# Splitting one float32 load of v in two, with its scalings, two w_out combinations and one turn put elsewhere in two queues

## The chip, the cores and the metric

One core of one Trainium2 chip runs the whole program. The metric is device time in microseconds (us), lower is better. The profile is of one execution of the same program, taken by the hardware profiler; its engines are PE (matmul), PEld (weight loads into PE), DVE (vector), ACT (activations), POOL (GpSimd) and SP (which computes nothing and issues DMAs).

## The reference

Retention over 4 sequences of 768 tokens with 8 heads of 64, then a feed-forward layer with a sine in it, over the 3072 tokens.

```python
gamma = 1.0 - 2.0 ** (-5.0 - np.arange(H))
for t in range(S):
    state = gamma * state + einsum('bhd,bhe->bhde', k[:, :, t], v[:, :, t])
    y[:, :, t] = scale * einsum('bhd,bhde->bhe', q[:, :, t], state)
x = y.transpose(0, 2, 1, 3).reshape(B * S, H * D)
h = x @ w_in                       # 512 -> 2048
s = np.sin(alpha * h)
out = (h + s * s / (alpha + 1e-09)) @ w_out
```

## The kernel before, in words

**Tiles and phases.** Each sequence is cut into 6 chunks of 128 tokens, 24 in all, and these are worked off in the order of the list `order` (L70 to L74), called `P` later. P[11], the twelfth tile, is chunk 3 of the second sequence (sequence 1 in the code); P[12] and P[13] are its chunks 4 and 5. P[14], P[15] and P[16] are chunks 1 to 3 of the third sequence (sequence 2), P[17] is chunk 1 of the fourth (sequence 3). The tiles form ten groups (4, then eight times 2, then 4). Phase g (`phase`, L908) runs, for the tiles of group g, the product with `w_in` (L617), the sine and the square on ACT (L620, L625) and the sum on DVE into `gT` (L632), while PE also runs the product with `w_out` of group g-1 (L641). A phase of two tiles has 8 slots, n = 0 to 7. A place such as (3, 5) is slot 5 of phase 3. Functions put on a place by `at` run in that slot in the order in which they were put there; those put there by `mixes` run behind it.

**The burst of a tile.** At fixed places PE interrupts the feed-forward work with a burst (`burst`, L465): the state's share of the old tile's output (L380), the scores of the new tile (L402, L406), the sum of k times v of the old tile into the state (L428), and the old tile's own share (L444). For a tile that is `wide` (L128: from chunk 3 of the second sequence on) L428 and L444 read `v_seq`, the scaled v; the scores read `qkT`, the turned q and k. Old and new tile of the bursts that matter here are P[10] and P[11] at (3, 1), P[11] and P[12] at (3, 5), P[12] and P[13] at (4, 1), P[13] and P[14] at (4, 5), P[14] and P[15] at (5, 1), P[15] with P[16] and P[17] at (5, 6). PE runs its instructions in the order written, so when one waits, all behind it wait.

**How q, k and v of a wide tile arrive.** `load_seq` (L131) loads one sequence, or a `part` of its wide tiles, with eight DMAs, one for each pair of a half and a head. q and k go through POOL's queue into `qk_seq` (as bfloat16), v goes through SP's queue into the float32 buffer `vf`. `scale_v` (L191) then multiplies v of one tile by its decays on POOL, `vf` to `v_seq` (L197). `turn` (L301) is a transposing DMA in SP's queue, `qk_seq` to `qkT` (L304). `mix_w` (L675) forms one piece of a sum or difference of two blocks of `w_out` on POOL (L686), needed from phase 7 on. SP also issues the stores of results, `out_dram<-o_sb` (L654).

**What sets the order.** Everything is written out by hand: the place table `where` and the calls of `at` decide at which point of the program an instruction is issued, and each engine runs its own in that order. A DMA waits, before it is issued, for the DMA that was issued eight before it on the same engine (eight semaphores go round on each of the two engines), and for the data that it reads. Nothing behind a waiting instruction on its engine goes ahead. The function `loads` (L1134), at (2, 2), is the part that the change takes apart.

Of the kernel before, what the change touches and what calls it, by code (L numbers as in the profile page):

```python
# [38 lines left out]
def kernel(  # L39
# [55 lines left out]
    def half(x):  # L95
        return slice(64 * x, 64 * x + 64)

    def head(b, m, e):
        return 4 * m + 2 * e + (e ^ b)
# [28 lines left out]
    def wide(j):  # L128
        return j >= NCH + 3 and j % NCH > 0

    def load_seq(bt, names="qkv", part=slice(None), between={}, some=slice(None)):  # L131

        cs = [c for c in range(NCH) if wide(bt * NCH + c)]
        nh = 2 * len(cs)
        if ("seq", bt) not in raw:
            raw["seq", bt] = (big.tile([128, nh, 2, NP, D], BF16, name=f"qk_seq{bt}", tag=f"qk_seq{bt}"),
                              big.tile([128, nh, NP, D], BF16, name=f"v_seq{bt}", tag=f"v_seq{bt}"))
        tqk, tv = raw["seq", bt]
        now = cs[part]
        fs = slice(2 * (now[0] - cs[0]), 2 * (now[-1] - cs[0]) + 2)  # L140
        if "v" in names and "vf" not in raw:
            raw["vf"] = work.tile([128, 16, NP, D], F32, name="vf", tag="gA", bufs=1)
        for name, src in (("q", q), ("k", k), ("v", v)):
            if name not in names:
                continue
            if name == "v":
                vf = raw["vf"][:, 6:16] if bt == 2 else raw["vf"][:, 0:nh]
                for i, c in enumerate(cs):
                    raw["vf", bt * NCH + c] = vf[:, 2 * i:2 * i + 2]
            for n, (b, m, e) in list(enumerate(heads))[some]:  # L150
                if n in between:
                    between[n]()
                r, at = half(b), 2 * m + e
                o = vf[r, fs, at, :] if name == "v" else tqk[r, fs, "qk".index(name), at, :]
                (nc.sync if name == "v" else nc.gpsimd).dma_start(out=o, in_=src[bt, head(b, m, e), now[0] * C:(now[-1] + 1) * C, :].rearrange("(f i) d -> i f d", i=64))  # L155
        for i, c in enumerate(cs):
            j, f = bt * NCH + c, slice(2 * i, 2 * i + 2)
            raw["qk", j], raw["k", j], raw["v", j] = tqk[:, f], tqk[:, f, 1], tv[:, f]
# [32 lines left out]
    def scale_v(j, eng):  # L191
        t, by = raw["v", j], kg
        o = t
        if wide(j):
            o, t = (x.rearrange("i f p d -> i (f p) d") for x in (t, raw["vf", j]))
            by = kgq
        eng.tensor_mul(o, t, by[:, j % NCH, :, None].to_broadcast([128, H, D]))  # L197
# [103 lines left out]
    def turn(j):  # L301

        st["qkT", j] = work.tile([128, 2 * NP, 128], BF16, name="qkT", tag="qkT", bufs=6)
        nc.sync.dma_start_transpose(out=st["qkT", j], in_=raw["qk", j].rearrange(  # L304
            "i a f p d -> i (a f p d)" if wide(j) else "i a h d -> i (a h d)"))
# [369 lines left out]
    def mix_w(eng, home):  # L675

        n, i, c = w_todo[home].pop(0)
        a, b, op = W_MIX[n]
        if home == "vr":
            to = big.tile([128, 2, NH], BF16, name="w_mix", tag="vr", bufs=11)  # L680
        else:
            if home not in w_home:
                w_home[home] = (consts if home == "dec" else big).tile(
                    [128, 2 if home == "dec" else 3, 4, NH], BF16, name="w_mix", tag="dec" if home == "dec" else "qk_seq1")
            to = w_home[home][:, (2 if home == "dec" else 3) - 1 - len(w_todo[home])]
        eng.tensor_tensor(to, w_block(*a, slice(i, i + c)), w_block(*b, slice(i, i + c)), op=op)  # L686
        for j in range(c):
            w_mix[n, i + j] = to[:, j]
# [262 lines left out]
    def X(j):  # L951
        return lambda: turn(j)
# [3 lines left out]
    P = order  # L956
# [122 lines left out]
    def pieces_w(n, home):  # L1079
        return lambda: [mix_w(nc.gpsimd, home) for _ in range(n)]  # L1080

    def scaled(*js):
        return lambda: [scale_v(j, nc.gpsimd) for j in js]
# [5 lines left out]
    where = {}  # L1089
# [8 lines left out]
    def at(place, fn):  # L1098
        atts[place[0]].setdefault(place[1], []).append(fn)

    def B(old, new, first, beside, second):

        return lambda: burst(old, new, first, beside=beside, second=second)

    for n in range(9, 17):
        new = P[n]
        first = new - 1 if new % NCH == 1 else None
        at(where[n], B(P[n - 1], new, first, P[17] if n == 16 else None, e3 if n == 15 else None))
        if n != 10:
            at({15: (4, 6), 16: (4, 5)}.get(n, where[n]), X(P[n + 2]))  # L1110
    for i, spot in ((16, (6, 4)), (18, (7, 4)), (20, (8, 1))):
        new = P[i + 2:i + 4] if i < 20 else P[22:23]
        at(spot, lambda i=i, new=new: pair(P[i:i + 2], new))
# [19 lines left out]

    def loads():  # L1134
        turn(P[12])
        load_seq(1, "v")
        pieces_w(2, "vr")()
        scale_v(P[10], nc.gpsimd)
        pieces_w(2, "vr")()
        load_seq(2, "q")  # L1140
        load_seq(2, "k", between={4: scaled(P[11]), 5: pieces_w(1, "vr"), 7: pieces_w(1, "vr")})
        scale_v(P[12], nc.gpsimd)
        scale_v(P[13], nc.gpsimd)
        load_seq(3, "qk", slice(0, 2))

    at((2, 2), loads)
    def mixes(place, fn):
        behind_slot.setdefault(place, []).append(fn)

# [2 lines left out]
    for spot in ((4, 0), (4, 2)):  # L1152
        mixes(spot, lambda: mix_w(nc.vector, "vr"))
    for spot, fn in (((3, 6), pieces_w(2, "dec")), ((3, 6), scaled(P[14], P[15], P[16])), ((4, 5), pieces_w(1, "vr")),
                     ((4, 5), pieces_w(3, "seq"))):
        mixes(spot, fn)
    for spot, m, only in (((6, 1), 0, "s"), ((6, 3), 2, "s"), ((6, 3), 0, "dx"), ((6, 3), 2, "d"), ((6, 5), 4, "s"), ((6, 5), 2, "x"),
                          ((6, 5), 4, "dx"), ((6, 7), 6, "s"), ((6, 7), 6, "dx")):
        mixes(spot, lambda m=m, only=only: mix_g(6, m, 2, nc.gpsimd, only))
# [38 lines left out]
```

## Time and profile before

| | us |
|---|---|
| median of the 3 runs shown | 210.84 |
| the 3 runs | 210.84, 205.76, 210.92 |
| the profiled execution | 206.72 |
| its span (first to last instruction) | 205.0 |
| PE busy in the span | 197.3 (96%) |
| POOL busy | 177.7 (87%) |
| DVE busy | 159.1 (78%) |
| ACT busy | 153.5 (75%) |

The profiled execution lies 0.96 above the lowest run and 4.12 below the median. All positions below are from the start of its span. A row of the timeline gives start, length, engine, line, operation, what is written from what, and how many instructions were merged; the brackets at its end give the engine's idle time before it and what ended that. "DMA to landing" is the time from the start of a DMA's issue to the moment its last byte is reported there.

### The profile page before, as it was taken

To read this page: it belongs to the slowest core of one execution; us is meant where nothing else is said; L and a number is where in the kernel's file an instruction comes from. 1 tells how busy PE (TensorE), PEld (TensorE's weight loads), DVE (VectorE), ACT (ScalarE), POOL (GpSimd) and SP (SyncE) were. 2 spreads that over 40 slices of the span, in tenths; PEclk is the share of its full clock that TensorE was granted. 3 is DMA by queue.
4 is the path that set the end of the run, shared out by engine and by line. 5 is a ranking of instruction groups with operands and counts; after the bars stand their busy time and mean duration, and the time that the engine had idled before them with its cause. 6 is when DMAs were issued, how large, how long until landed. Compare 5 with 4: busy or idle time off the path is not lost.

```text
span 205.0 us, 6219 instructions
## 1 busy us (share of the span) xinstructions
PE 197.3 (96%) x2503; PEld 136.3 (67%) x2503; DVE 159.1 (78%) x340; ACT 153.5 (75%) x316; POOL 177.7 (87%) x212
## 2 busy tenths in 40 slices
PE   7889999999999999699999999999999999999994
PEld 7545544467776666466766666768888885555983
DVE  5788499877999977578788787796799896577853
ACT  7779788557997787667876959788777979999120
POOL 8999986999999799899999999899997997997000
DMA  8999999999999989999999799995063111001123
GB/s 131 151 181 193 199 201 175 167 131 129 109 184 186 115 153 146 208 166 109 183 172 225 79 131 186 187 213 133 25 80 83 28 51 56 0 0 51 54 102 102
DMA packets 104348, 26.52 MB, mean 129 GB/s; under 512 B 93648, under 2 KB 102528, under 8 KB 104320
## 3 DMA queue, kind: packets, MB, share of 16 engines
q0 software_dynamic: 66384, 11.67, 76.3%
q1 hardware_dynamic: 37936, 14.47, 35.7%
q8 instruction: 19, 0.31, 0.7%
q14 instruction: 9, 0.07, 0.2%
HBM read 27.30 MB, written 6.29 MB: 164 GB/s over the span
## 4 chain that ended last, share of the span: by engine, by line
PE 71%; DVE 14%; DMA 5%; ACT 4%; POOL 3%; issue 2%; SPq 0%; POOLq 0%; DVEq 0%
PE ph L617 32%; PE po L641 20%; DVE gT L632 6%; PE a L765 6%; DMA out_dram<-o_sb 3%; PE b L765 3%; PE ab L765 3%; DMA qkr<-in_k_dram 2%; ACT s L620 2%; ACT s L625 1%; PE c L765 1%; POOL qkr L125 1%; DVE xT L502 1%; DVE aTw L414 1%; PE py L380 1%
## 5 line engine op out<-in xcount | busy, mean ns | idle before, releaser
L632 DVE SCALAR_TENSOR_TENSOR gT<-s,rec_alpha,ph 128x256 bf16<-128x256 f32 (+3 forms) x164 | 79.5, 522 | 25.8 <-ACT s L625 24.4
L617 PE MATMUL ph<-xT,w_in 128*128 128x256 bf16 (+3 forms) x656 | 98.3, 291 | 0.4 <-DVE o_sb L651 0.2
L620 ACT ACTIVATE s<-ph,alpha_sb 128x256 f32<-128x256 f32 (+3 forms) x164 | 75.8, 505 | 26.0 <-PE ph L617 25.4
L617 PEld LDWEIGHTS <-w_in 128*128 128x128 bf16 x656 | 63.0, 98 | 27.2 <-issue 1.2
L625 ACT ACTIVATE s<-s 128x512 f32<-128x512 f32 (+1 forms) x94 | 58.7, 626 | 2.8
L641 PE MATMUL po<-w_out,gT 128*128 128x512 bf16 x224 | 58.3, 380 | 0.0
L719 POOL TENSOR_TENSOR g_mix<-gT 128x512 bf16<-128x512 bf16 (+1 forms) x51 | 49.2, 997 | 4.2 <-DVE gT L632 2.9
L641 PEld LDWEIGHTS <-gT 128*128 128x128 bf16 x224 | 20.4, 98 | 16.5 <-DVE gT L632 0.5
L155 POOL DMA_DIRECT2D qk_seq<-in_k_dram x32 | 21.5, 742 | 2.6 <-DMA qk_seq<-in_q_dram 2.5
L765 PEld LDWEIGHTS <-g_mix 128*128 128x128 bf16 x208 | 19.5, 98 | 4.7
L155 POOL DMA_DIRECT2D qk_seq<-in_q_dram x32 | 21.5, 725 | 0.0
L686 POOL TENSOR_TENSOR w_mix<-w_out 128x512 bf16<-128x512 bf16 (+1 forms) x13 | 20.0, 1606 | 0.0
L197 POOL TENSOR_TENSOR v_seq<-vf,kgq 128x512 bf16<-128x512 f32 x13 | 13.8, 1093 | 0.0
L125 POOL DMA_DIRECT2D vr<-in_v_dram x11 | 10.3, 934 | 1.5 <-DMA w_in<-in_moe_w_in_dram 1.3
L414 DVE TENSOR_TENSOR aTw<-pa,maskq 128x768 bf16<-128x768 f32 x10 | 9.6, 955 | 1.9 <-PE pa L428 1.7
L899 PE MATMUL spare<-warm 128*128 128x112 bf16 (+1 forms) x54 | 8.2, 324 | 1.2 <-DVE warm L207 1.2
L502 DVE TENSOR_TENSOR xT<-py,qg 128x512 bf16<-128x512 f32 x13 | 8.9, 685 | 0.5 <-PE py L460 0.5
L765 PEld LDWEIGHTS <-gT 128*128 128x128 bf16 x88 | 7.9, 98 | 1.9
L651 DVE COPY o_sb<-po 128x512 f32<-128x512 f32 x11 | 7.6, 690 | 1.6 <-PE po L641 1.1
L765 PE MATMUL a<-w_mix,gT 128*128 128x256 bf16 (+1 forms) x72 | 8.7, 261 | 0.0
L398 DVE TENSOR_TENSOR aT<-pa,mask 128x1024 bf16<-128x1024 f32 x7 | 8.5, 1220 | 0.1
L765 PE MATMUL b<-w_out,g_mix 128*128 128x256 bf16 x64 | 8.5, 273 | 0.0
(135 smaller groups left out, 225.2 us busy)
## 6 DMA issues: line engine op xcount, KB each, us to landing
out_dram<-o_sb SPq DMA_DIRECT2D x21, 256.0 KB, 4.4
w_in<-in_moe_w_in_dram POOLq DMA_DIRECT2D x8, 256.0 KB, 7.8
w_out<-in_moe_w_out_dram POOLq DMA_DIRECT2D x8, 256.0 KB, 8.1
vf<-in_v_dram SPq DMA_DIRECT2D x16, 96.0 KB, 4.4
vr<-in_v_dram POOLq DMA_DIRECT2D x11, 128.0 KB, 5.8
vf<-in_v_dram SPq DMA_DIRECT2D x8, 128.0 KB, 6.0
qkr<-in_q_dram POOLq DMA_DIRECT2D x7, 128.0 KB, 5.8
qkr<-in_k_dram POOLq DMA_DIRECT2D x7, 128.0 KB, 5.4
```

The costliest lines, as they stand in the source:

```text
L125: nc.gpsimd.dma_start(out=t, in_=chunk_of(src, j))
L155: (nc.sync if name == "v" else nc.gpsimd).dma_start(out=o, in_=src[bt, head(b, m, e), now[0] * C:(now[-1] + 1) * C, :].rearrange("(f i) d ...
L197: eng.tensor_mul(o, t, by[:, j % NCH, :, None].to_broadcast([128, H, D]))
L414: return {"mask": lambda: nc.vector.tensor_mul(aT, pa[:, :, 0:384].rearrange("p e (m t) -> p e m t", m=2), maskq[:, None, None, :].to_broa ...
L617: nc.tensor.matmul(self.ph[:, m, :], w_in[:, i, f * 128:(f + 1) * 128], xT[g][:, i, self.lo:self.hi], start=(m == 0 and i == 0), stop=(i = ...
L620: nc.scalar.activation(out=self.s[:, m, :], in_=self.ph[:, m, :], func=ACTF.Sin, scale=alpha_sb[:, f:f + 1])
L625: nc.scalar.activation(out=self.s, in_=self.s, func=ACTF.Square)
L632: nc.vector.scalar_tensor_tensor(gT[self.g][:, f, self.lo:self.hi], self.s[:, m, :], rec_alpha[:, f:f + 1], self.ph[:, m, :], op0=ALU.mult ...
L641: nc.tensor.matmul(po[g, ts], gT[g][:, f, ts * C:(ts + 1) * C], w_out[:, f, :], start=(f == 0), stop=(f == FF - 1))
L686: eng.tensor_tensor(to, w_block(*a, slice(i, i + c)), w_block(*b, slice(i, i + c)), op=op)
L719: eng.tensor_tensor(o, i0, i1, op=op)
L765: nc.tensor.matmul(t, self.left(n, j), r, start=k not in self.begun, stop=(j == FH - 1), skip_group_check=True)
```

## The change

The load of v of the second sequence, eight DMAs for its three wide tiles at once, becomes two loads of eight DMAs: P[11] alone at the old point, P[12] and P[13] together in a new function `more_loads` at (3, 1). On POOL the scaling of P[11] moves from behind the fourth to behind the first of the eight k loads of the third sequence; two pieces of `w_out`'s combinations move from between those k loads to behind the scaling of P[12], and both lie, with the scaling of P[13] and the first loads of the fourth sequence, in `more_loads`. The turn of P[15], the sixteenth, moves from (4, 1) to (3, 5), next to that of P[14].

```diff
-            at({15: (4, 6), 16: (4, 5)}.get(n, where[n]), X(P[n + 2]))
+            at({13: (3, 5), 15: (4, 6), 16: (4, 5)}.get(n, where[n]), X(P[n + 2]))
...
     def loads():
         turn(P[12])
-        load_seq(1, "v")
+        load_seq(1, "v", slice(0, 1))
         pieces_w(2, "vr")()
         scale_v(P[10], nc.gpsimd)
         pieces_w(2, "vr")()
         load_seq(2, "q")
-        load_seq(2, "k", between={4: scaled(P[11]), 5: pieces_w(1, "vr"), 7: pieces_w(1, "vr")})
+        load_seq(2, "k", between={1: scaled(P[11])})
+
+    def more_loads():
+        load_seq(1, "v", slice(1, None))
         scale_v(P[12], nc.gpsimd)
+        pieces_w(2, "vr")()
         scale_v(P[13], nc.gpsimd)
         load_seq(3, "qk", slice(0, 2))

     at((2, 2), loads)
+    at((3, 1), more_loads)
```

SP, from the turns of P[11] and P[12] (the first row) on. `qk_seq_1193` is q and k of the second sequence, `qk_seq_1359` those of the third; a `vf` row of 64x6 is three tiles, of 64x4 two, of 64x2 one. Before:

```order
L304 DMA_TRANSPOSE qkT<-qk_seq_1193 128x8x128 x2
L155 DMA vf<-in_v_dram 64x6x64 x8
L654 DMA out_dram<-o_sb 128x512 x2
L304 DMA_TRANSPOSE qkT<-qk_seq_1193 128x8x128
L654 DMA out_dram<-o_sb 128x512
L304 DMA_TRANSPOSE qkT<-qk_seq_1359 128x8x128
L155 DMA vf<-in_v_dram 64x6x64 x8
L654 DMA out_dram<-o_sb 128x512
L304 DMA_TRANSPOSE qkT<-qk_seq_1359 128x8x128
```

After the change:

```order
L304 DMA_TRANSPOSE qkT<-qk_seq_1193 128x8x128 x2
L155 DMA vf<-in_v_dram 64x2x64 x8
L654 DMA out_dram<-o_sb 128x512 x2
L304 DMA_TRANSPOSE qkT<-qk_seq_1193 128x8x128
L155 DMA vf<-in_v_dram 64x4x64 x8
L654 DMA out_dram<-o_sb 128x512
L304 DMA_TRANSPOSE qkT<-qk_seq_1359 128x8x128 x2
L155 DMA vf<-in_v_dram 64x6x64 x8
```

Eight loads of P[12]'s and P[13]'s v now stand behind the turn of P[13], and both turns of the third sequence (P[14], P[15]) ahead of that sequence's v.

POOL, from the loads of the third sequence's q on. `v_seq_1194` is the scaled v of the second sequence (P[11], P[12], P[13] in turn), `v_seq_1360` of the third; `qk_seq_1384`, after the change `qk_seq_1662`, is q and k of the fourth. Before:

```order
L155 DMA qk_seq_1359<-in_q_dram 64x10x64 x8
L155 DMA qk_seq_1359<-in_k_dram 64x10x64 x4
L197 TENSOR_TENSOR v_seq_1194<-vf,kgq 128x512
L155 DMA qk_seq_1359<-in_k_dram 64x10x64
L686 TENSOR_TENSOR w_mix<-w_out 128x512
L155 DMA qk_seq_1359<-in_k_dram 64x10x64 x2
L686 TENSOR_TENSOR w_mix<-w_out 128x512
L155 DMA qk_seq_1359<-in_k_dram 64x10x64
L197 TENSOR_TENSOR v_seq_1194<-vf,kgq 128x512 x2
L155 DMA qk_seq_1384<-in_q_dram 64x4x64 x8
L155 DMA qk_seq_1384<-in_k_dram 64x4x64 x8
```

After the change:

```order
L155 DMA qk_seq_1359<-in_q_dram 64x10x64 x8
L155 DMA qk_seq_1359<-in_k_dram 64x10x64
L197 TENSOR_TENSOR v_seq_1194<-vf,kgq 128x512
L155 DMA qk_seq_1359<-in_k_dram 64x10x64 x7
L197 TENSOR_TENSOR v_seq_1194<-vf,kgq 128x512
L686 TENSOR_TENSOR w_mix<-w_out 128x512 x2
L197 TENSOR_TENSOR v_seq_1194<-vf,kgq 128x512
L155 DMA qk_seq_1662<-in_q_dram 64x4x64 x8
L155 DMA qk_seq_1662<-in_k_dram 64x4x64 x8
L686 TENSOR_TENSOR w_mix<-w_out 128x1024 x2
L197 TENSOR_TENSOR v_seq_1360<-vf,kgq 128x512 x3
```

P[11]'s scaling stands three k loads earlier, the k loads are not interrupted any more, and P[12]'s scaling is the first instruction behind them; no instruction but eight DMAs of v on SP was added. The number and order of PE's, ACT's and DVE's instructions are the same in both programs.

## Prediction

> **What bounds the kernel now.** I read the page first: the shares of the engines and the chain that ended last.
>
> ```profile
> PE 197.3 (96%) x2503; PEld 136.3 (67%) x2503; DVE 159.1 (78%) x340; ACT 153.5 (75%) x316; POOL 177.7 (87%) x212
> PE 71%; DVE 14%; DMA 5%; ACT 4%; POOL 3%; issue 2%; SPq 0%; POOLq 0%; DVEq 0%
> ```
>
> PE is busy almost throughout and carries most of the chain. So an idle time of PE counts in full, and only that counts. Next I looked in the chain, in order of time, for the pieces that are not PE, DVE or ACT. Between 80 and 87 us stands a pair (start, length):
>
> ```profile
> 80.09 5.27 DMA out_dram<-o_sb
> 85.37 1.07 POOL v_seq L197
> ```
>
> PE's timeline at the same place is the burst at (3, 5), which needs P[11]'s scaled v:
>
> ```profile
> 84.67 0.20 PE L406 MATMUL pa<-qkT 64*64 64x64 bf16 x4
> 86.48 0.32 PE L428 MATMUL pa<-v_seq,qk_seq 64*64 64x64 bf16 x16 [1.62 <-POOL v_seq L197]
> ```
>
> PE sat idle for 1.62. That is the stall that the change touches, and 1.62 is the most that this place can give. Then the two queues, SP and POOL, from there to the next tiles' scalings:
>
> ```profile
> 73.89 5.43 SPq L155 DMA_DIRECT2D vf<-in_v_dram  x8
> 79.43 1.03 SPq L654 DMA_DIRECT2D out_dram<-o_sb  x2
> 80.51 1.98 SPq L304 DMA_TRANSPOSE qkT<-qk_seq  x1
> 82.61 1.22 SPq L654 DMA_DIRECT2D out_dram<-o_sb  x1
> 95.30 1.24 SPq L304 DMA_TRANSPOSE qkT<-qk_seq  x1
> 96.59 5.38 SPq L155 DMA_DIRECT2D vf<-in_v_dram  x8
> 102.73 1.38 SPq L304 DMA_TRANSPOSE qkT<-qk_seq  x1
> ```
>
> ```profile
> 75.89 5.77 POOL L155 DMA_DIRECT2D qk_seq<-in_q_dram  x8
> 81.56 2.24 POOL L155 DMA_DIRECT2D qk_seq<-in_k_dram  x3
> 84.65 0.71 POOL L155 DMA_DIRECT2D qk_seq<-in_k_dram  x1 [0.85 <-DMA qk_seq<-in_q_dram]
> 85.37 1.06 POOL L197 TENSOR_TENSOR v_seq<-vf,kgq 128x512 bf16<-128x512 f32 x1
> 86.36 0.76 POOL L155 DMA_DIRECT2D qk_seq<-in_k_dram  x1
> 87.13 1.16 POOL L686 TENSOR_TENSOR w_mix<-w_out 128x512 bf16<-128x512 bf16 x1
> 88.23 1.59 POOL L155 DMA_DIRECT2D qk_seq<-in_k_dram  x2
> 89.83 1.17 POOL L686 TENSOR_TENSOR w_mix<-w_out 128x512 bf16<-128x512 bf16 x1
> 90.94 0.73 POOL L155 DMA_DIRECT2D qk_seq<-in_k_dram  x1
> 91.68 2.05 POOL L197 TENSOR_TENSOR v_seq<-vf,kgq 128x512 bf16<-128x512 f32 x2
> 93.67 4.95 POOL L155 DMA_DIRECT2D qk_seq<-in_q_dram  x8
> 98.54 4.99 POOL L155 DMA_DIRECT2D qk_seq<-in_k_dram  x8
> 103.37 4.39 POOL L686 TENSOR_TENSOR w_mix<-w_out 128x1024 bf16<-128x1024 bf16 x2
> 107.55 3.19 POOL L197 TENSOR_TENSOR v_seq<-vf,kgq 128x512 bf16<-128x512 f32 x3
> ```
>
> The reader is to see that POOL has one gap of 0.85 in these 35 us and otherwise runs from instruction to instruction. The last row is the scaling of P[14], P[15] and P[16], begun not when their v lands but when POOL comes to it. PE reads these results here:
>
> ```profile
> 94.27 0.30 PE L428 MATMUL pa<-v_seq,qk_seq 64*64 64x64 bf16 x16
> 109.89 0.23 PE L402 MATMUL pa<-qkT 64*64 64x128 bf16 x4
> 110.07 0.30 PE L428 MATMUL pa<-v_seq,qk_seq 64*64 64x64 bf16 x16
> ```
>
> 94.27 needs P[12]'s v, 110.07 needs P[14]'s. P[12] is scaled by 92.7 (half of the 2.05), so PE has 1.6 in hand there; P[14] by 108.61 (a third of the 3.19), so it has 1.46. POOL's later order is thus nearly as tight as the stall itself. Last, the landings of single DMAs, from the views of the tiles and of DMA issues in narrow windows: the eight v loads from 73.89; eight one-tile v loads at 113 to 118, when POOL issues no load; eight two-tile v loads at 119 to 126, beside loads by POOL; the turn of P[13] from 80.51; that of P[14] from 95.30; that of P[15] from 102.73; the last k load of the third sequence, from 90.94; and the share of POOL's DMA queue from 70 to 96.
>
> ```profile
> DMA to landing us min/median/max: 2.6/3.7/6.5
> ...
> DMA to landing us min/median/max: 2.1/2.2/2.7
> ...
> DMA to landing us min/median/max: 3.0/4.0/5.5
> ...
> qkT<-qk_seq SPq DMA_TRANSPOSE x1, 10.2
> ...
> qkT<-qk_seq SPq DMA_TRANSPOSE x1, 4.1
> ...
> qkT<-qk_seq SPq DMA_TRANSPOSE x1, 6.5
> ...
> qk_seq<-in_k_dram POOLq DMA_DIRECT2D x1, 80.0 KB, 4.0
> ...
> q0 software_dynamic: 12390, 1.55, 99.7%
> ```
>
> The DMA engines have a backlog around 80 to 92: the same kind of turn takes 10.2 there and 4.1 later.
>
> **The change part by part.** *P[11]'s v alone.* Still eight issues, of the 5.43 that the present eight take, so the last goes out at 78.6, but with a third of the bytes. Landing after 2.7 (the slowest of the one-tile loads) to 3.7 (the median of the present ones) gives 81.3 to 82.3. On POOL the scaling now comes behind eight q loads (to 81.66) and one k load (2.24/3 = 0.75): 82.3. With 1.06 it ends at 83.4. PE is at this place at 84.67 + 0.20 = 84.87. So the stall goes: **-1.62**. It would come back only if the landing slipped by 1.5.
>
> *P[12]'s and P[13]'s v.* On SP these eight follow two stores and the turn of P[13]: the turn ends at 82.4, eight issues at the 5.4 of the SP rows end at 87.8, the last starts at 87.1. But that last one is the eighth DMA behind the turn of P[13], so it waits for the turn's landing as well. The turn took 10.2 behind 768 KB of v and two stores; now a third of that v is ahead of it, while POOL's loads run on uninterrupted. Its landing lies between 80.5 + 4.1 = 84.6 and 80.5 + 10.2 = 90.7; I take the middle, 87.6. So the last v load starts at about 87.6 and lands after 3.0 to 5.5. Since POOL's k loads are in flight at the same time I take 4.4, above the median: 92.0. The ends are 87.1 + 2.2 = 89.3 and 90.7 + 4.0 = 94.7.
>
> *POOL.* Behind P[11]'s scaling seven k loads of 0.73 end at 88.5. Then POOL comes to P[12]'s scaling and waits for 92.0: a new idle time of 3.5 in a queue that had 0.85. The scaling ends at 93.0. PE, 1.62 earlier than before, wants it at 92.65: **+0.4**. Behind it on POOL stand the two pieces of w_out (1.16 + 1.17), P[13]'s scaling (1.03), sixteen loads, two larger pieces and P[14]'s scaling. The loads begin at 96.4 instead of 93.67, so all of this is 2.7 later: P[14]'s scaling begins at 107.55 + 2.7 = 110.25 and ends at 111.3. PE, at 110.07 - 1.62 + 0.4 = 108.85, waits **+2.45**. The two pieces themselves cost nothing on the way, since they lie ahead of P[14]'s scaling in both programs; the gap costs, and it is all of the difference.
>
> *The turn of P[15].* Before, it landed at 102.73 + 6.5 = 109.2 for a use at 109.89, only 0.7 in hand. Now it goes out behind that of P[14], some six us earlier: that margin grows, cost nothing. Its issue of 1.38 delays the v of P[14] to P[16], which waits behind it on SP. The turn of P[14] waits for the last k load: issued by 88.5, it lands after 4.0 or more, 92.5 to 96.7 (8.2 if it meets the backlog of the turn of P[13]). At the late end the two turns end at 99.3, the eight v loads at 104.7, and the last lands within 5.5, at 109.5. That is still ahead of the 110.25 at which POOL comes to it, so POOL's delay covers this part; without that delay it would itself hold P[14] until then.
>
> *Sum.* -1.62 + 0.4 + 2.45 = **+1.23** at the burst at (5, 1). Behind it I expect no more: POOL is then 1.4 later against PE than before, and it catches up where it waits for DVE today, 2.9 in three waits:
>
> ```profile
> POOL g_mix L719 <- DVE gT L632: 2.9, 3, 1.3
> ```
>
> The span of 205.0 becomes 206.2, the profiled execution's 206.72 becomes 207.95. That execution is 4.12 below the median of the runs shown, which lie at two levels, one at 205.76 and two at 210.9. On the median, 210.84 + 1.23 = **212.1**. This is within 2%, about what a measurement of this kernel can tell from no change.
>
> **The rivals.** *A, the full gain.* The v loads of P[12] and P[13] land with little but a fixed delay: the turn ahead lands by 87 because most of the v is out of its way, and the last load, issued at 87.1, lands after 2.2, as the one-tile loads do at 113. Then POOL idles from 88.5 to 89.3, no more than the 0.85 that it idles today; P[12] is ready at 90.4, P[14] at 108.61, for a PE that wants it at 108.45: gain 1.62 - 0.16 = 1.46, so 209.4. For it: 512 KB less in the way of everything issued until 82. Against it: the 2.2 was measured with POOL's queue empty, the two-tile loads beside POOL's loads took 4.0, and POOL's queue is 99.7% busy here. The Trainium skill's page "DMA: Bandwidth & Descriptors", section "Anatomy of one DMA — SWDGE (gpsimd) path", puts a DMA at about 2.0 us and its bytes at 436 GB/s (fitted there to loads issued by GpSimd), an estimate of 2.2 us for 64 KB; by that rule rival A is the result. The 4.0 of the two-tile loads does not agree with it where another queue is loaded.
>
> *B, a late turn.* The turn of P[13] keeps its 10.2 since the k loads take the place of the v that has left. The last v load then starts at 90.7 and lands at 94.7. P[12] is ready at 95.75, PE stands from 92.65: +3.1, 1.5 later than before. P[14]: POOL idles 6.2 instead of 0.85, its scaling ends at 108.61 + 5.35 = 113.96, 3.9 behind 110.07: 214.7. For it: the present turn of P[13] is the slowest DMA of the stage. It is slower than 2% (4.2) from a landing after 95.0 on. The same page, section "Queues, rings and completion order", states that each DMA engine goes round between the queues that have work for it; then a fuller POOL queue slows SP's, which is the direction of B. No run here shows that arbitration by itself.
>
> *C, nothing moves.* P[11]'s v lands no sooner, because q loads ahead of it hold it to 84.5 as the slowest present v load does (the seventh, issued at 73.89 + 6 x 0.68 = 78.0, 6.5 later): PE's stall stays, and POOL waits early instead of late, with the same sum: 210.8. Against it: the bytes in SP's queue are a third.
>
> **How the numbers follow.** The forecast (a new wait at P[12] and P[14], +0.3 to +3.0) has 0.58, A 0.25, B 0.12, C 0.05. For the forecast alone the range is 211.1 to 213.8. With A and B, and with both levels of the runs (206.72 - 1.46 = 205.3 below, 210.92 + 3.9 = 214.8 above), I give 205.5 to 214.5. No case gains 2%; for runs that fall on different levels (5.1 apart, 2.4%) I leave 0.03 to faster, and 0.07 to slower, mostly B's tail. Within 2%: 0.90.
>
> **What would show it.** Right: no wait of L428 for `v_seq` at 84.9; P[11]'s scaling near 82.3; an idle time of POOL of 2 or more ahead of the next `v_seq`, ended by the `vf` DMA; a new wait of PE for `v_seq` in the burst near 109, longer than that near 93. The forecast is wrong if POOL shows no such gap, if P[14]'s scaling starts by 108, or if PE still waits near 85. The turn's landing near 87.6 decides between the forecast, A and B.

## The result and the profile after

The changed kernel is slower: 213.01 us, the median of four runs (212.1 to 213.38), against 208.98 for the kernel before in the same comparison (205.76 to 210.92). The ratio is 1.031 [1.023, 1.039]; it is formed without the two runs of before at 210.8 and 210.9. The forecast was 212.1 and "within 2%".

The profiled execution took 213.22 with a span of 211.4, against 206.72 and 205.0. That is +6.4, and the trace has all of it in one stage. Starts of PE's bursts (L380), in us, worked out from PE's timeline of both kernels:

| burst | before | after | difference |
|---|---|---|---|
| (3, 5) | 84.39 | 84.65 | +0.26 |
| (4, 1) | 93.96 | 92.69 | -1.27 |
| (4, 5) | 101.72 | 108.19 | +6.47 |
| (5, 1) | 109.64 | 116.10 | +6.46 |
| (5, 6) | 118.40 | 124.87 | +6.47 |

From (3, 5) to (4, 1) the change gains 1.53. From (4, 1) to (4, 5) it loses 7.74. Behind that nothing moves any more.

The page of the changed kernel, the lines that answer to those first shown of before (busy time; the granted clock of PE, which is the share of its full clock that the throttle lets through, in tenths over 40 slices of 5.3 us; the chain by engine):

```profile
PE 200.2 (95%) x2503; PEld 137.2 (65%) x2503; DVE 158.9 (75%) x340; ACT 153.4 (73%) x316; POOL 177.7 (84%) x212
PEclk9999999999999999996699999999999999999999
PE 72%; DMA 11%; DVE 6%; POOL 6%; ACT 2%; issue 1%; SPq 0%; POOLq 0%; DVEq 0%
```

PE was busy 2.9 longer with the same 2503 matmuls: two slices near 100 us ran at a lower clock. And the DMA share of the chain went from 5% to 11%. The chain in order of time (start, length) names the transfers:

```profile
80.88 9.08 DMA qkT<-qk_seq
89.98 6.61 DMA vf<-in_v_dram
96.76 1.05 POOL v_seq L197
98.59 1.82 PE po L641 x4
```

So: the turn of P[13], then the last v load of P[12] and P[13], which starts at 89.98 as the turn lands at 89.96, then P[12]'s scaling, then PE. PE's timeline at (3, 5), (4, 1) and (5, 1):

```profile
85.21 0.32 PE L428 MATMUL pa<-v_seq,qk_seq 64*64 64x64 bf16 x16
97.85 0.43 PE L428 MATMUL pa<-v_seq,qk_seq 64*64 64x64 bf16 x16 [4.68 <-POOL v_seq L197]
98.53 1.89 PE L641 MATMUL po<-w_out,gT 128*128 128x512 bf16 x4
101.92 1.92 PE L641 MATMUL po<-w_out,gT 128*128 128x512 bf16 x4
104.62 1.03 PE L641 MATMUL po<-w_out,gT 128*128 128x512 bf16 x4
116.53 0.30 PE L428 MATMUL pa<-v_seq,qk_seq 64*64 64x64 bf16 x16
```

The stall at (3, 5) is gone. A new one of 4.68 stands at (4, 1), and behind it each group of four matmuls takes 1.9 until 103.6, then 1.03 again. From L428 of (4, 1) to (4, 5) PE took 108.19 - 97.85 = 10.34, before 101.72 - 94.27 = 7.45: 2.89 more. With the later start (97.85 - 92.69 against 94.27 - 93.96, 4.85) this is the 7.74. At (5, 1) there is no wait. The windows (stretch, length, busy time of PE, PEld, DVE, ACT, POOL, then the clock) show the clock at 0.55 behind the stall, with 55 matmuls; before (second row), the same stretch had 1.00 and 96 matmuls:

```profile
98.00:104.50 6.50, 6.50 (x55) 3.57 (x51) 3.47 (x8) 1.76 (x4) 6.50 (x9) 0.55 0.87 140
98.00:104.50 6.50, 6.50 (x96) 4.43 (x95) 5.49 (x12) 4.76 (x11) 6.50 (x11) 1.00 1.70 186
```

SP's queue and POOL, from the v load of P[11] on:

```profile
74.43 5.29 SPq L155 DMA_DIRECT2D vf<-in_v_dram  x8
79.81 1.02 SPq L654 DMA_DIRECT2D out_dram<-o_sb  x2
80.88 2.97 SPq L304 DMA_TRANSPOSE qkT<-qk_seq  x1
83.91 6.67 SPq L155 DMA_DIRECT2D vf<-in_v_dram  x8
97.99 2.64 SPq L304 DMA_TRANSPOSE qkT<-qk_seq  x2
```

```profile
84.12 1.04 POOL L197 TENSOR_TENSOR v_seq<-vf,kgq 128x512 bf16<-128x512 f32 x1 [0.97 <-DMA out_dram<-o_sb]
85.11 5.04 POOL L155 DMA_DIRECT2D qk_seq<-in_k_dram  x7
96.75 1.04 POOL L197 TENSOR_TENSOR v_seq<-vf,kgq 128x512 bf16<-128x512 f32 x1 [6.60 <-DMA vf<-in_v_dram]
97.76 2.25 POOL L686 TENSOR_TENSOR w_mix<-w_out 128x512 bf16<-128x512 bf16 x2
114.82 3.21 POOL L197 TENSOR_TENSOR v_seq<-vf,kgq 128x512 bf16<-128x512 f32 x3
```

POOL sits 6.60 ahead of P[12]'s scaling, with two pieces of `w_out` behind it that it could have formed meanwhile. P[14]'s scaling starts 7.27 later than before. Where a bracket of L197 names `out_dram`, a store, it is v that the scaling waits for: a store shares its semaphore with a v load, and the store issued at 79.81 landed 5.0 later, at 84.8, behind the start at 84.12. Last, the landings, from the view of DMA issues in narrow windows (KB each, median us to landing):

```profile
vf<-in_v_dram SPq DMA_DIRECT2D x8, 32.0 KB, 2.4
qkT<-qk_seq SPq DMA_TRANSPOSE x1, 9.1
vf<-in_v_dram SPq DMA_DIRECT2D x8, 64.0 KB, 6.6
qk_seq<-in_k_dram POOLq DMA_DIRECT2D x7, 80.0 KB, 7.2
```

P[11]'s small loads land in a median of 2.4; what is issued from 80.9 to 90, by SP or POOL, has medians of 6.6 to 9.1. Of the eight second v loads only the last waits for the turn's landing. Yet the others land behind it too: the first, issued at 83.91, after 6.6, at 90.5, and the seventh, issued at 88.19, after 7.2, at 95.4. So the last one's wait puts P[12]'s v off by 1.2 at most (96.6 against 95.4).

### The profile page after: what moved, and what is told of

It is laid out like the page before. It is cut to its first block, busy times and chain, and to the rows that moved or that the text cites. A ratio compares the mean times of both kernels' runs of the same rounds, so it can differ in the third digit from the quotient of the medians.

```text
span 211.4 us, 6231 instructions
## 1 busy us (share of the span) xinstructions
PE 200.2 (95%) x2503; PEld 137.2 (65%) x2503; DVE 158.9 (75%) x340; ACT 153.4 (73%) x316; POOL 177.7 (84%) x212
## 4 chain that ended last, share of the span: by engine, by line
PE 72%; DMA 11%; DVE 6%; POOL 6%; ACT 2%; issue 1%; SPq 0%; POOLq 0%; DVEq 0%
PE ph L617 33%; PE po L641 20%; PE a L765 6%; DMA qkT<-qk_seq 4%; DMA w_out<-in_moe_w_out_dram 3%; DMA vf<-in_v_dram 3%; POOL qkr L125 3%; PE ab L765 2%; PE b L765 2%; DVE gT L632 2%; POOL vr L125 2%; PE c L765 1%; ACT s L620 1%; DVE aTw L414 1%; PE py L380 1%; PE pt L298 1%
## 5 line engine op out<-in xcount | busy, mean ns | idle before, releaser
L617 PE MATMUL ph<-xT,w_in 128*128 128x256 bf16 (+3 forms) x656 | 99.3, 293 | 0.2
L617 PEld LDWEIGHTS <-w_in 128*128 128x128 bf16 x656 | 63.7, 99 | 27.9 <-issue 2.1
L641 PE MATMUL po<-w_out,gT 128*128 128x512 bf16 x224 | 60.0, 389 | 0.1
L641 PEld LDWEIGHTS <-gT 128*128 128x128 bf16 x224 | 20.9, 99 | 17.3 <-issue 1.1
L197 POOL TENSOR_TENSOR v_seq<-vf,kgq 128x512 bf16<-128x512 f32 x13 | 13.8, 1097 | 7.6 <-DMA vf<-in_v_dram 6.6
L765 PEld LDWEIGHTS <-gT 128*128 128x128 bf16 x88 | 7.9, 98 | 1.9
```

What stands on the lines that cost most here:

```text
L617: nc.tensor.matmul(self.ph[:, m, :], w_in[:, i, f * 128:(f + 1) * 128], xT[g][:, i, self.lo:self.hi], start=(m == 0 and i == 0), stop=(i = ...
L641: nc.tensor.matmul(po[g, ts], gT[g][:, f, ts * C:(ts + 1) * C], w_out[:, f, :], start=(f == 0), stop=(f == FF - 1))
L765: nc.tensor.matmul(t, self.left(n, j), r, start=k not in self.begun, stop=(j == FH - 1), skip_group_check=True)
```

## The experiments

The theory after this profile: the second v load lands late because it stands behind the slow turn of P[13] and beside POOL's k loads; PE's wait for it then lowers the clock, which adds to it. The rivals: POOL's new order is the cause; the moved turn of P[15] is; the clock fell for a reason of its own. Diffs are against the changed kernel where nothing else is said. All ratios are to the kernel before on the same chip.

### Is it the late v, and what makes it late?

**The turn of P[13] earlier**, next to that of P[12], ahead of the first v load:

```diff
-        if n != 10:
+        if n not in (10, 11):
...
         turn(P[12])
+        turn(P[13])
         load_seq(1, "v", slice(0, 1))
```

> The changed kernel with the turn of P[13] issued right behind those of P[11] and P[12], ahead of P[11]'s v, instead of at (3, 1). Theory (the second load of v is late because it stands behind that turn and behind the backlog): the turn goes out near 74, lands near 78, the eight loads of the second v start near 82 and land by 91, PE waits less than 1 for v_seq near 93 and its clock stays at full rate; time 205 to 207. Rival 'POOL's order' (P[12]'s scaling behind all k loads is the cost, wherever the v is): 213 as the changed kernel. Rival 'k loads alone hold the v': it lands near 94, a wait of 2 to 3, 208 to 210.

Measured: 209.45 (207.13 to 210.83) against 208.93, ratio 1.005 [0.999, 1.011]. PE's waits for `v_seq` and POOL's scalings of P[12] and P[14]:

```profile
85.56 0.32 PE L428 MATMUL pa<-v_seq,qk_seq 64*64 64x64 bf16 x16 [0.53 <-POOL v_seq L197]
111.11 0.32 PE L428 MATMUL pa<-v_seq,qk_seq 64*64 64x64 bf16 x16 [1.79 <-POOL v_seq L197]
```

```profile
91.55 1.04 POOL L197 TENSOR_TENSOR v_seq<-vf,kgq 128x512 bf16<-128x512 f32 x1 [1.04 <-DMA out_dram<-o_sb]
109.85 3.20 POOL L197 TENSOR_TENSOR v_seq<-vf,kgq 128x512 bf16<-128x512 f32 x3
```

With the turn out of the way P[12] is scaled 5.2 sooner, the wait at (4, 1) and the half rate are gone, and the ratio to the kernel before falls from 1.031 to 1.005. The turn itself, issued at 73.83 there, lands after 3.2. The time is above the 205 to 207 expected; what is left stands at (5, 1): 1.79 for P[14], which POOL reaches late.

**The v load ahead of the turn of P[13]** instead, with the turn left in the stage: `X(P[13])` is placed at (3, 1) behind `more_loads`.

```diff
-        if n != 10:
+        if n not in (10, 11):
...
     at((3, 1), more_loads)
+    at((3, 1), X(P[13]))
```

> The changed kernel with the second load of v ahead of the turn of P[13] on SP instead of behind it. Theory (the turn, slow beside loads, is what holds the v): the v lands near 90 and PE does not wait for v_seq near 93; the turn goes out near 86.5 and lands 93 to 95, so PE waits 0.5 to 2.5 for the scores instead, at full clock; 207 to 209. Rival 'k loads alone hold the v': it lands after 93 as well, 210 to 213.

Measured: 208.9 (207.46 to 211.44) against 208.93, ratio 1.005 [1.001, 1.010].

```profile
94.78 0.25 PE L402 MATMUL pa<-qkT 64*64 64x128 bf16 x4 [1.35 <-DMA qkT<-qk_seq]
112.85 0.32 PE L428 MATMUL pa<-v_seq,qk_seq 64*64 64x64 bf16 x16 [1.49 <-POOL v_seq L197]
```

Now the turn is the late one (L402 reads `qkT`), and P[12]'s v is in time: the two swap places. From both runs the order of turn and v in SP's queue decides the wait of 4.68.

**The turn of P[15] back at (4, 1)**, as before:

```diff
-            at({13: (3, 5), 15: (4, 6), 16: (4, 5)}.get(n, where[n]), X(P[n + 2]))
+            at({15: (4, 6), 16: (4, 5)}.get(n, where[n]), X(P[n + 2]))
```

> The changed kernel with the turn of P[15] back at (4, 1). Theory: the wait near 93 (4.7) and the slow stretch behind it are as in the changed kernel, since this turn goes out behind all of it; 212 to 214. Rival (two turns in a row are what delays SP's queue): 209 or less.

Measured: 211.55 (210.91 to 213.44) against 209.05, ratio 1.021 [1.009, 1.032].

```profile
96.42 0.32 PE L428 MATMUL pa<-v_seq,qk_seq 64*64 64x64 bf16 x16 [2.38 <-POOL v_seq L197]
```

The wait stays (here 2.38, with slow matmuls behind it until 100), so this turn doesn't make it; it goes out behind all of it, at 99.35 in the changed kernel. That the wait is shorter here has two parts: P[12]'s scaling starts at 95.32 instead of 96.75, and PE comes 0.9 later, after a wait of 1.15 for P[11].

**POOL in its old order**, with v still loaded in two parts:

```diff
-        load_seq(2, "k", between={1: scaled(P[11])})
+        load_seq(2, "k", between={4: scaled(P[11]), 5: pieces_w(1, "vr"), 7: pieces_w(1, "vr")})
...
         scale_v(P[12], nc.gpsimd)
-        pieces_w(2, "vr")()
```

> The changed kernel with POOL's order around the k loads as before (P[11]'s scaling behind the fourth k load, the two pieces of w_out between them); v stays split and the turn of P[15] stays at (3, 5). Theory (the second load of v is late by itself): P[12]'s v still lands after 94, PE waits 2 to 4.5 near 95 and 0.5 to 1.5 near 86; 211 to 214. Rival 'POOL's order': without the new order no wait beyond that of the kernel before; 207 to 209.

Measured: 211.0 (209.86 to 212.48) against 209.05, ratio 1.017 [1.006, 1.028].

```profile
87.50 0.43 PE L428 MATMUL pa<-v_seq,qk_seq 64*64 64x64 bf16 x16 [2.92 <-POOL v_seq L197]
98.07 0.32 PE L428 MATMUL pa<-v_seq,qk_seq 64*64 64x64 bf16 x16 [1.11 <-POOL v_seq L197]
```

P[12]'s v is late whatever POOL does ahead of it (its scaling starts at 96.98 here, at 96.75 in the changed kernel). P[11]'s v is late here too: its last load, issued at 80.54, lands after 5.5, at 86.0, just as POOL has issued the k loads ahead of the scaling.

**The v load whole again**, with POOL's new order and the moved turn kept:

```diff
-        load_seq(1, "v", slice(0, 1))
+        load_seq(1, "v")
...
     def more_loads():
-        load_seq(1, "v", slice(1, None))
         scale_v(P[12], nc.gpsimd)
```

> The changed kernel with the v of P[11], P[12] and P[13] loaded at once as before; POOL's new order and the turn of P[15] at (3, 5) stay. Theory: the v of P[12] is in by 86, so there is no wait near 93; P[11]'s v lands as late as before, so PE waits 0.5 to 1.6 near 85; time 205.5 to 207.5. Rival 'POOL's order': still a wait of several us near 93, 211 to 213.

Measured: 208.38 (207.42 to 211.5) against 208.93, ratio 1.006 [1.000, 1.012]. PE's waits, and POOL's scalings of P[14] to P[16]:

```profile
86.36 0.32 PE L428 MATMUL pa<-v_seq,qk_seq 64*64 64x64 bf16 x16 [1.26 <-POOL v_seq L197]
112.03 0.32 PE L428 MATMUL pa<-v_seq,qk_seq 64*64 64x64 bf16 x16 [1.91 <-POOL v_seq L197]
110.94 3.04 POOL L197 TENSOR_TENSOR v_seq<-vf,kgq 128x512 bf16<-128x512 f32 x3
```

There is 1.26 for P[11], nothing at (4, 1), and 1.91 for P[14], with a clock of 0.72 from 112 to 118. So the split of v brings the 4.68, and the wait at (5, 1) comes without the split, from POOL's new order: POOL has no idle time right ahead of P[14]'s scaling, it comes to it late.

### The clock behind a wait

**Sixteen idle matmuls** of 512 columns on zeros, written to a bank of PE's output memory that the next burst overwrites, ahead of the burst with P[12] as the new tile; they fill the wait and add no result:

```diff
         py = st["py", j]
+        for _ in range(16 if j == P[12] else 0):
+            nc.tensor.matmul(py[0], warm[:, :128], warm[:, :512], start=True, stop=True)
```

> The changed kernel with 16 matmuls of 512 columns on zeros (16 x 0.216 = 3.5 us) ahead of the burst of P[12], into a bank that the burst then overwrites; the v arrives as in the changed kernel. They fall into the 4.7 in which PE waits. Theory (the long wait lowers PE's granted clock for some 6 us, which costs 2.9 on top of the wait): the wait left is about 1.2, the clock stays at full rate, 210.1. Rival (the slow stretch has another cause, such as DMA traffic on the same memory): the slow stretch stays, 213.

Measured: 212.99 (211.25 to 217.38) against 208.93, ratio 1.024 [1.014, 1.035]. Its profiled execution, 217.38, had a clock of 0.95 from 10 to 115 us, and of 0.51 for 3.5 us behind a wait of 1.81 at (5, 1). The other three had mean clocks of 0.999, 0.991 and 0.998, the four of the changed kernel 0.984 to 0.990. A second profiled execution:

> e5_fill once more, for a profile at full clock. Theory: no slow stretch near 98 to 104, the wait near 93 under 1.5, but a wait of 1 to 2 near 116, since P[14]'s scaling is still late by POOL's gap; 211 to 212.

Measured: 214.27, span 212.5. The matmuls (15 of the 16 are in the trace), the bursts at (4, 1), (4, 5) and (5, 1), and the stretch that had 0.55 (the two lines added make L380 and L428 to L382 and L430):

```profile
93.31 3.62 PE L375 MATMUL py<-warm 128*128 128x512 bf16 x15
97.71 0.32 PE L430 MATMUL pa<-v_seq,qk_seq 64*64 64x64 bf16 x16 [0.38 <-POOL v_seq L197]
105.19 0.31 PE L382 MATMUL py<-qkT,s_q 64*64 64x128 bf16 x8
115.97 0.32 PE L430 MATMUL pa<-v_seq,qk_seq 64*64 64x64 bf16 x16 [2.25 <-POOL v_seq L197]
```

```profile
98.00:104.50 6.50, 6.34 (x63) 4.26 (x52) 5.27 (x11) 4.08 (x10) 6.50 (x10) 1.00 1.03 168
```

v is as late as in the changed kernel (L430 at 97.71, against 97.85), but PE idles only 0.38 and the clock stays at 1.00: the wait itself lowered it. (4, 5) then starts at 105.19, 3.0 sooner. Yet nothing is gained at the end: P[14]'s scaling starts at 114.70, as in the changed kernel, so PE waits 2.25 for it and ends that wait at 115.97, where the changed kernel stood at 116.53. So the half rate cost 0.56 net there: POOL, held up 6.6 by the late v, was nearly as late as the slowed PE. And behind the new wait the clock is at 0.50 from 117.39 to 120.80, so that the loss is made again there.

**The same on the kernel before**, ahead of the burst at (3, 5), once with 7 matmuls (1.5 us) and once with 14 (3.0 us); diffs as above, with `P[11]`.

> The kernel before with 7 matmuls of 512 columns on zeros (1.5 us) ahead of the burst of P[11], inside the 1.62 in which PE waits near 85. Theory (waits of PE near 2 us also lower its granted clock in part of the executions, and that spreads the times of the kernel before from 206 to 212): the wait left is under 0.5, the granted clock is 1.0 in nearly all runs, and the median falls to 206 to 207.5. Rival (the spread has another cause): the same spread, median 208 to 209.

Measured with 7: 208.14 (206.18 to 211.08) against 209.05, ratio 0.998 [0.993, 1.004]; the clock was 0.99 in four of ten runs all the same. This tells nothing apart.

> The kernel before with 14 matmuls of 512 columns on zeros (3.0 us) ahead of the burst of P[11]. They cost PE about 1.4 where the wait is 1.62, and leave none in executions where it would be up to 3. Theory (the slower executions of the kernel before are those in which this wait grows and the clock then falls): granted clock 1.0 in all runs, all within 207.5 to 208.5. Rival (the clock falls for another reason): clocks of 0.98 to 0.99 in a third of the runs, times up to 212.

Measured with 14: 208.57 (207.88 to 209.42) against 207.45 (205.31 to 212.46, 21 runs), ratio 1.011 [1.004, 1.017]. The clock was 1.0 in all four runs; in the 21 of before it lay below 0.993 in ten, which took 208.4 to 212.5, and at 0.998 or more in the eleven others, 205.3 to 207.5. They fit the theory that the spread of the kernel before comes from its own wait near 85, which lowers the clock in some executions. They don't show it: four runs are few, 7 matmuls left four low clocks in ten, and the profiled execution of the kernel before is one at full clock.

### Is there an order that keeps the gain?

**P[14] scaled sooner**: the kernel with the early turn, and P[14]'s scaling between the two large pieces of `w_out`.

```diff
-    for spot, fn in (((3, 6), pieces_w(2, "dec")), ((3, 6), scaled(P[14], P[15], P[16])), ((4, 5), pieces_w(1, "vr")),
+    for spot, fn in (((3, 6), pieces_w(1, "dec")), ((3, 6), scaled(P[14])), ((3, 6), pieces_w(1, "dec")), ((3, 6), scaled(P[15], P[16])), ((4, 5), pieces_w(1, "vr")),
```

> The kernel with the early turn of P[13] (e1_turn14_early), and P[14]'s scaling put between the two large pieces of w_out's combinations instead of behind both. Theory (what is left there is POOL's order: P[14]'s scaling came 1.79 too late for the burst at (5, 1)): the scaling starts 2.1 sooner, no wait near 109 over 0.3, PE's clock stays at full rate in nearly every run; 1.8 less than e1_turn14_early at full clock, that is 205.5 to 206.5, and below the kernel before by 0.5 to 2.5 in the median. Rival (P[14]'s v is not in before that): the wait stays over 1, 207.5.

Measured: 209.97 (209.53 to 210.45) against 209.05, ratio 1.012 [1.002, 1.022]. The wait at (5, 1) is gone, as expected; the time isn't:

```profile
87.85 0.43 PE L428 MATMUL pa<-v_seq,qk_seq 64*64 64x64 bf16 x16 [2.79 <-POOL v_seq L197]
```

P[11]'s v came later here than in the kernel that it was made from (scaled from 86.76 instead of 84.47), with the same order up to that place. The delay is older than the stage: the last k load of the second sequence, which the turn of P[11] needs, was issued at 69.02 and took 3.9 to land (there 68.41 and 2.4), so the turn went out at 73.13 instead of 71.10, and P[11]'s v loads behind the turns from 77.22 instead of 75.20. Why that k load took longer is open.

**All of v at (2, 0)**, ahead of the turns of P[11] and P[12]; then the same with P[14] scaled sooner as above:

```diff
-        load_seq(1, "v", slice(0, 1))
...
-        load_seq(1, "v", slice(1, None))
...
+    at((2, 0), lambda: load_seq(1, "v"))
```

> The changed kernel with the whole v of P[11] to P[13] loaded in one piece at (2, 0), ahead of the turns of P[11] and P[12], at 62 to 67, where SP waits for nothing but the k loads of the second sequence; POOL's new order and the turn of P[15] stay. Theory (every stall here is a scaled v that comes late, through its load or through POOL's order): P[11]'s and P[12]'s scalings run without a wait of POOL, PE does not wait near 85 and 93, under 0.5 near 109; clock at full rate; 205 to 206.5 in nearly all runs. Rival (the backlog only moves): the turn of P[11] lands after 76.7 and PE waits 1 to 3 for it at (3, 1); 207 to 209.

> As e12_v_at_20, with P[14]'s scaling between the two large pieces of w_out's combinations. Theory: the rest of the wait near 109 goes too; the same or 0.2 to 0.5 less than e12_v_at_20. Rival: the large piece that moves behind is needed, no gain.

Measured: 208.37 (206.96 to 210.74), ratio 1.006 [1.001, 1.010], and 207.05 (205.61 to 210.18), ratio 1.001 [0.995, 1.007], both against 207.45. No wait at (3, 5) or (4, 1) in either; in exchange the turn of P[11] is late (0.97 and 1.39 near 79), P[14] costs 1.83 and 1.11 near 112, and in the second POOL is late for `g_mix` (1.23 at 145.78).

**P[11]'s v at (2, 0), the rest at the old point**, ahead of the turn of P[13]; then the same with P[14] scaled sooner:

```diff
-        load_seq(1, "v", slice(0, 1))
+        load_seq(1, "v", slice(1, None))
...
-        load_seq(1, "v", slice(1, None))
...
+    at((2, 0), lambda: load_seq(1, "v", slice(0, 1)))
```

> As e15_v12_at_20_v15, with P[14]'s scaling behind both large pieces, as in the changed kernel. Theory: no waits near 85 and 93, a wait of 0.2 to 1.8 near 109, so most of the 1.6 is given back there: 205.5 to 207.5, above e15_v12_at_20_v15. Rival (POOL's order there does not matter): the same as e15_v12_at_20_v15.

> The changed kernel with P[11]'s v alone loaded at (2, 0), P[12]'s and P[13]'s v at the old point ahead of the turn of P[13], and P[14]'s scaling between the two large pieces of w_out's combinations. Theory (the three stalls near 85, 93 and 109 are all there is, each passed on to the next when one is removed; a third of the v ahead of the turns costs them little): none of the three waits over 0.6, clock at full rate, 1.0 to 1.6 below the full-clock runs of the kernel before: 205 to 206, and no run over 208. Rival (another cost of the split or of POOL's new order remains that the stalls do not show): 207 or more at full clock.

Measured: 206.66 (205.6 to 208.4) and 209.15 (208.11 to 209.93), both against 208.64 (205.91 to 213.33); the ratios are 1.001 [0.996, 1.006] and 1.013 [1.002, 1.024]. The first has the lowest median of all versions, with a clock of 0.998 or more in all ten runs; in the ratio it gains nothing. Its trace says why:

```profile
109.97 0.32 PE L428 MATMUL pa<-v_seq,qk_seq 64*64 64x64 bf16 x16 [1.63 <-POOL v_seq L197]
```

Its bursts start at 84.30, 92.06, 99.82 and 107.73, so 1.9 ahead of before at the last two; then PE waits 1.63 for P[14]'s v, and (5, 6) starts at 118.31 against 118.40. In the second, POOL idled 3.38 for that v and PE 2.12: asked for sooner, it wasn't there sooner. There POOL was also late for `g_mix` (1.26 at 144.99), as in the other version with this order.

**The v of P[14] to P[16] ahead of its turns**, at (3, 4), on the first of these two; then also with P[14] scaled sooner:

```diff
-    for spot, bt, part in (((3, 6), 2, slice(0, 3)), ((4, 6), 3, slice(0, 1)), ((5, 2), 2, slice(3, None)), ((6, 0), 3, slice(1, None))):
+    for spot, bt, part in (((3, 4), 2, slice(0, 3)), ((4, 6), 3, slice(0, 1)), ((5, 2), 2, slice(3, None)), ((6, 0), 3, slice(1, None))):
```

> As e14_v12_at_20, with the v of P[14] to P[16] loaded at (3, 4), ahead of the turns of P[14] and P[15], while SP waits for the k loads of the third sequence, instead of behind them at (3, 6). Theory (the 1.6 of the first stall is passed on at each later place where a scaled v comes late; in e14_v12_at_20 POOL waited 1.36 for this very load and PE 1.63): POOL does not wait for that v, PE waits under 0.6 near 108, the clock is full in nearly all runs, 0.8 to 1.6 below e14_v12_at_20 and below the full-clock runs of the kernel before: 204.5 to 206. Rival (a further cost of the split or of POOL's new order): no gain on e14_v12_at_20, 206 to 207; or the load delays the k loads and the turn of P[14], and a wait for qkT appears near 100.

> As e16_v15_v_at_34, with P[14]'s scaling between the two large pieces of w_out's combinations. Theory: up to 0.5 less than e16_v15_v_at_34, no wait near 108. Rival: POOL is late further on, a wait for g_mix near 145 as in the two versions that had this order; the same time or more.

Measured: 210.18 (206.42 to 211.35) and 210.33 (207.4 to 212.9), both against 208.28; for the second the ratio is 1.008 [1.003, 1.013].

```profile
103.40 0.30 PE L402 MATMUL pa<-qkT 64*64 64x128 bf16 x4 [3.18 <-DMA qkT<-qk_seq]
```

No wait for `v_seq` is left, and the turn of P[14] is late instead, by 3.18 and 3.74. The last k load that it reads, in the first of the two issued at 89.26, landed at 98.95.

Of these seven versions only the one with 206.66 came out within the time expected of it; in the others a wait was left, or came up at another place.

## Why the prediction was wrong

**The stall at (3, 5): right in size, not in its margin.** The term was -1.62, and the trace shows 1.53 less up to (4, 1) and no wait. But P[11]'s scaling ended at 85.16, not at 83.4, and PE read it at 85.21: the seventh of the small loads took 5.1 and landed at 83.56, beyond the 81.3 to 82.3 given, and POOL started the scaling at 84.12, not 82.3. The early turn's run, with 0.53, shows the margin used up.

**P[12]'s v: the step that failed.** The prediction took the middle for the turn's landing, 87.6, and 4.4 for the load behind it, and got 92.0 and +0.4. The turn took 9.08 and landed at 89.96. The load took 6.61, beyond the 3.0 to 5.5 of the rows, and landed at 96.59; the wait was 4.68. That the last load waits for the turn's landing was right, but it is the smaller part: the loads that don't wait for it took 6.2 to 7.2, and the seventh landed at 95.4, where the prediction's latest end for the last one was 94.7. The prediction let the turn act through the wait of one load alone; the runs show that the loads of this stage are slow themselves, a median of 6.2 even where they are issued ahead of the turn, from 80.3 on. The row of 4.0 came from 119 to 126 us, where POOL's loads were there too but no turn; it was no measure of this stage. The 10.2 of the old turn and the 99.7% of POOL's queue were, and rival B rested on them. Moving two thirds of v behind the turn left the turn as slow and put the v into the worst place. The Trainium skill's page "DMA: Bandwidth & Descriptors", section "Anatomy of one DMA — SWDGE (gpsimd) path", has figures, fitted to loads issued by GpSimd, from which the prediction worked out an estimate of 2.2 for 64 KB; the 6.2 to 7.2 here don't agree with it.

**The clock: a term that was missing.** No part of the prediction has PE run slower behind a wait; it put this at nothing without a reason. In the changed kernel it is 2.89 from (4, 1) to (4, 5), and the filled wait shows its cause. Its net part at (5, 1) was 0.56, since POOL was late as well.

**POOL's order: right, but covered.** The prediction passed POOL's idle time on to P[14]: +2.7 on its scaling and a wait of 2.45. POOL idled 6.60, and the scaling came 7.27 later. In the changed kernel PE didn't wait for it, because PE was 6.5 late itself by then; with the half rate taken away it waited 2.25, with the late v taken away 1.79. So at (5, 1) the loss was in hand twice, by PE and by POOL, and to take one away alone gave little. The sign that the prediction gave, a wait near 109 longer than that near 93, came out the other way round: 4.68 near 93 and none at (5, 1).

**The rivals.** B was what happened, only more: POOL idle 6.60 (6.2), last load started 89.98 (90.7), landed 96.59 (94.7), PE waiting 4.68 (3.1), P[14] scaled by 115.87 (113.96). Its price of +3.9 becomes 5.8 with a landing 1.9 later, and P[14] scaled by 115.87 is 5.8 behind the 110.07 of before; PE's half rate goes with the rest of the 6.47. It had 0.12 and should have had the most. A, by which v lands after little but a fixed delay, is excluded by the 6.6. C is too, since the first stall did go.

**Sum.** On the profiled executions, -1.53 + 7.74 + 0.26 (already there ahead of the change's stage) = 6.47, against a forecast of 1.23. The 7.74 is 4.85 of waiting and 2.89 of slower matmuls. That the median of 213.01 lies within the forecast's own 211.1 to 213.8 is luck: the sum was added to 210.84, the median of three runs at two levels, and from the profiled execution it gave 207.95, where 213.22 was measured.

## What to carry to other kernels

A transfer moved to remove one wait has to be priced in the stage where it lands, with the latencies that this stage's own rows show, not those of the same transfer elsewhere; and the DMA issued eight behind it on the same engine waits for its landing. Where the DMA engines have a backlog, as here around 80 to 92 us, each order makes another transfer late (here v of P[11], v of P[12], the turn of P[13], v of P[14] or the turn of P[14]), and no version was shown to be faster than the kernel before. A wait of PE of about two us is worth removing twice over, since the clock may fall behind it; and a gain must be followed up to the next tile that the same engine prepares.

## What the runs showed of the hardware

How long a wait of PE must be before the granted clock falls, over the profiled executions from 60 to 195 us: behind all waits up to 1.79 it stayed as it was (1.62, 1.63 and 1.79 are the longest). Behind 1.81, 1.83, 1.91, 2.25, 2.38, 2.79, 2.92, 3.18, 3.74 and 4.68 the clock is at 0.50 for 3.41 each, and for twice that, 6.83, at the 4.68 (97.04 to 103.87). The slow stretch begins between 0.8 ahead of the wait's end (at the 4.68) and 1.4 behind it (at the 2.25, from 117.39). One wait of 2.12 (the kernel with P[11]'s v at (2, 0) and P[14] scaled sooner) had no such stretch. The Trainium skill's page "TensorE: Matmul & The Clock Gate", section "What's actually happening", puts the fall after an idle window of about 3.4; here it followed waits from 1.81 on.

The 64 KB loads of v took a median of 6.6 behind the turn of P[13] at 84 to 90 us, and 3.7 in the version that issues them at 75, ahead of it. That P[11]'s v varied by two us between executions with the same order up to there (its scaling from 84.47 or 86.76) goes back to one k load, which landed after 2.4 or 3.9; why it did stays open.
